# Triangular solves on VectorE alone, and 320 zero products left out, in a delta-rule attention and mixture-of-experts kernel

## The chip, the cores and the metric

One core of one Trainium2 chip. The metric is the device time in microseconds (us) of one execution, and the time of a kernel is the median of several. Engine names: PE is TensorE (PEld its weight loads), DVE is VectorE, ACT is ScalarE, POOL is GpSimd, SP is SyncE (SPq is its queue of DMA starts). L448 is line 448 of the kernel before; lines of the changed kernel are named as such.

## The reference

Three stages follow one another. First a delta-rule attention over 4 batches x 8 heads, 768 tokens, head size 48:

```
for t in range(S):
    y[:, :, t] = einsum('bhd,bhde->bhe', q[:, :, t], state)
    v_old = einsum('bhde,bhd->bhe', state, k_n[:, :, t])
    state = state + beta_t * einsum('bhd,bhe->bhde', k_n[:, :, t], v[:, :, t] - v_old)
```

`k_n` is `k` divided by its norm. Then its output (3072 tokens of 384) goes through a mixture of 8 experts with a greedy assignment (each expert takes 384 tokens; two products with a relu between), and last through a dense layer pair with `h * sigmoid(h)` between, 384 to 2048 to 384.

## The kernel before, in words

The attention is computed in 24 chunks of 32 tokens, all 32 heads together (4 blocks of 32 partitions x 8). Inside a chunk the recurrence over 32 tokens becomes a triangular system, whose inverse is computed for a group of 4 chunks at once. There are 6 groups (`GROUPS`), so 6 solves.

- `prep` (L371 loads, L373 on ACT, L374 on DVE, L379 DMAs within SBUF) and `gram` (L396 on PE, then L403 on ACT, L405 on DVE, L409 on ACT, and L410 on DVE or POOL) make a chunk's Gram matrices in high and low halves.
- `tgroup` makes a group's inverse: two transposes (L421), norms (L426 to L441, with two scalings by L439), the first values of X (L448), a mask and the diagonal (L451 and L454, always on POOL), and then 30 rounds of a multiplication (L462) and an addition (L465). Round j takes n columns of X by m = 31 - j elements, each instruction reads what the one before it wrote, and the columns are cut between DVE and POOL by the table `SPLIT`, so that each engine runs its own chain of 60 instructions (fewer on POOL). Two transposes (L468) end the solve, then L475 on ACT and L477 on DVE or POOL write the result for each of the 4 chunks. X and the temporary exist once, so solves follow one another.
- `stage(c)` loads chunk c's keys and values (L485), converts (L488 on ACT, L489 on DVE), scales the values (L492 on DVE or POOL), and moves all operands of the chunk within SBUF by four DMAs (L497) into one of two buffers `rsl`. It waits for the chunk's inverse.
- `step(c)` is the recurrence over chunks: PE products L519 (values), L527 (keys by state), L537 (queries by state), L548 (inverse), L563 (state), L574 (output), with L502 on ACT and L503 on DVE after the first, the inverse and the state product (5 L503 of a chunk), L507 to L510 for halves made by PE, and after every second chunk four DMAs L586 that write the output.
- `gate(c)` makes the gate's logits (L595, L599 or L600 and L602, L608, and L614 after chunk 19 and after chunk 23).

After the attention come the expert search (L924 to L1034) and the experts' products (`mm`, L1138).

The order of all instructions is set when the kernel is built, by a list scheduler (`Plan`): every operation has a cost and a priority, operations with two engines in their cost table (L410, L477, L492, L804 and others) are given to one of them, and each engine then runs its list strictly in that order. At the beginning `shapes` puts 320 products of zeros on PE in several shapes, and `warm` has 300 more products of zeros (L192) at the lowest priority, which the scheduler puts where it takes PE to be idle.

Of the kernel before, what the change touches and what calls it, by code (L numbers as in the profile page):

```python
# [20 lines left out]
C = 32  # L21
# [10 lines left out]
N6 = 3  # L32
FH = 0.0
KF = 2
SPLIT = (
    (("DVE", 0, 6), ("Pool", 6, C)),
    (("DVE", 0, 5), ("Pool", 5, C)),
    (("DVE", 0, 4), ("Pool", 4, C)),
    (("DVE", 0, 5), ("Pool", 5, C)),
    (("DVE", 0, 4), ("Pool", 4, C)),  # L40
    (("DVE", 0, 10), ("Pool", 10, C)),
)
GROUPS = tuple(tuple(range(c, c + 4)) for c in range(0, NCH, 4))
SX, SWG = 6, 10

# [143 lines left out]
def warm(P, nc, bank, z, n, r, w):  # L189

    for _ in range(n):
        P.op("PE", WC, lambda e: nc.tensor.matmul(bank[:, 0:256], z[:, 0:128], z[:, 128:], start=True, stop=True),  # L192
             r=r, w=w, prio=-1e6, look=(1.0, 0.0))


def shapes(P, nc, banks, z, r, w):

    T = nc.tensor
    forms = (
        (1, lambda i: (slice(0, 128), slice(0, 128), 0)),  # L200
        (2, lambda i: (slice(64 * i, 64 * i + 64), slice(64 * i, 64 * i + 64), 0)),
        (2, lambda i: (slice(64 * i, 64 * i + 64), slice(0, 128), i)),
        (4, lambda i: (slice(32 * i, 32 * i + 32), slice(32 * i, 32 * i + 32), 0)),
        (2, lambda i: (slice(0, 128), slice(64 * i, 64 * i + 64), 0)),
    )

    for n, (k, form) in enumerate(2 * forms):
        def go(e, n=n, k=k, form=form):
            for j in range(32):
                rows, cols, b = form(j % k)  # L210
                at = 48 * (j // k % 8)
                T.matmul(banks[b][cols, at:at + 48], z[rows, 0:cols.stop - cols.start], z[rows, 128:176], start=True, stop=True)
        P.op("PE", 1.0, go, r=r, w=w, prio=HOT)


class Arena:


# [43 lines left out]
def act(n, sb=True):  # L262
    return 0.055 + 0.00083 * n + (0.043 if sb else 0.0)
# [10 lines left out]
def attention(tc, P, ar, sh, kq, kv, bt, cst, idh, wg, xs):  # L274
    nc = tc.nc
    V, A, G, T = nc.vector, nc.scalar, nc.gpsimd, nc.tensor
    E = {"DVE": V, "Pool": G}
# [29 lines left out]
    wz = ar.new(["wz"], [384], F16)  # L307
# [14 lines left out]
    def sta(t, at, Q):  # L322
        return t[:, at, Q // 4].rearrange("p s (i q) -> p (s i) q", q=4)[:, :, Q % 4]
# [12 lines left out]

    P.op("DVE", 0.2, lambda e: V.memset(wz, 0.0), w=["wz"])
    P.op("Pool", 0.1, lambda e: G.memset(tiny, 1e-30), w=["tiny"])
    shapes(P, nc, ar.banks[4:6], wz, ["wz"], [("y", 0), ("y", 1)])
    warm(P, nc, ar.banks[5], wz, WARM, ["wz"], [("y", 1)])  # L340
    P.op("DVE", 4.3, fill(gsl, "p x c g s n -> p (x c g s n)"), w=["gsl"])
    for t, k in ((rsl[1][:, 0:8], 1), (rsl[1][:, 8:], 1), (rsl[0][:, 0:8], 0), (rsl[0][:, 8:], 0)):
# [40 lines left out]
    def gram(c):  # L383
# [8 lines left out]
        def mm(e, Q):  # L392
            n = 0
            for t in range(2):
                for a, b in P3:
                    T.matmul(gp_[:, Q], sta(gs[:, x], 2 * a + t, Q), cv[:, :, b, t, Q // 4, :, Q % 4], start=(n == 0), stop=(n == 5))  # L396
                    n += 1
# [15 lines left out]
    def tgroup(g):  # L413
# [24 lines left out]
        for k in range(2):  # L438
# [3 lines left out]
             r=["nb0"], w=["nb1"])  # L442
        parts = [(k, en, k0, k1) for k, (en, k0, k1) in enumerate(SPLIT[g])]
        xk = [("X", k) for k in range(2)]
# [61 lines left out]
    def split_pe(hi, lo, acc, ident, s, n, kp, kh, kl):  # L506
        P.op("ACT", act(n, False), lambda e: A.activation(hi, acc, AF.Copy, scale=s), r=[kp], w=[kh])  # L507
        P.op("PE", 0.01 + n / 2400, lambda e: T.matmul(acc, ident, hi, start=False, stop=True, skip_group_check=True),
             r=["idl", kh], w=[kp])
        P.op("ACT", act(n, False), lambda e: A.activation(lo, acc, AF.Copy, scale=s), r=[kp], w=[kl])  # L510

    def step(c):
        x = c % 2
        rs, y = rsl[x], yp[x]
        for g in range(2):
            w_, u_, n_, wu_, st_ = wt[g], ut[g], ns[g], wu[g], st[g]

            def vin(e, g=g, wu_=wu_):
                T.matmul(wu_[:, 0], ids, kr[x][:, 8 + 4 * g:12 + 4 * g, :], start=True, stop=(c == 0))  # L519

            P.op("PE", 0.38, vin, r=["ids", ("kv", x, 0)], w=[("wu", g)], prio=LEAD["vin"])
            if c:
                def kn(e, bs, last, g=g, wu_=wu_, n_=n_):
                    for a, b in bs:
                        for Q in range(4):
                            for t in range(2):
                                T.matmul(wu_[:, 0, Q], sta(rs, KR[x] + 2 * a + t, 4 * g + Q), n_[:, b, t, Q, :],  # L527
                                         start=False, stop=(last and (a, b) == P3[-1] and Q == 3 and t == 1))
# [178 lines left out]
HOT = 1000.0  # L707
# [511 lines left out]
def _program(ins):  # L1219
    import concourse.bacc as bacc  # L1220

    nc = bacc.Bacc("TRN2", target_bir_lowering=False, num_devices=1)
    d = {k: nc.dram_tensor(f"in_{k}", a.shape, mybir.dt.from_np(a.dtype), kind="ExternalInput").ap()
         for k, a in ins.items()}
    out = nc.dram_tensor("out_0", _OUT, F32, kind="ExternalOutput").ap()
    with tile.TileContext(nc) as tc, ExitStack() as ctx:
        dram = ctx.enter_context(tc.tile_pool(name="dram", bufs=1, space=DRAM))
        xs = dram.tile([NTOK, 2 * DM], F16, name="xs")
        plan = Plan()
        ar = Arena(ctx, tc, plan, 212832)  # L1230
        ar.at(210852)
        sh = shared_tiles(ar)
        ar.at(0)
        plan.base, plan.look = 9.0 * HOT, LOOK
        attention(tc, plan, ar, sh, d["kq"], d["kv"], d["bt"], d["cst"], d["idl"], d["wg"], xs)
        moe(tc, plan, ar, sh, xs, d["w1"], d["w2"], d["win"], d["wout"], d["mch"], out)
        with tc.manual_schedule():
            plan.emit()
    return nc
# [22 lines left out]
```

## Time and profile before

| what | us |
|---|---|
| median of 3 runs | 1064.65 (1058.99 to 1065.28) |
| profiled execution, its own time | 1064.36 |
| its span in the trace | 1062.7 |
| outside the span | 1.66 |
| DVE busy over the span | 719.7 (68%) |
| POOL busy over the span | 395.8 (37%) |
| PE busy over the span | 935.5 (88%) |

Busy time is of instructions that work; a share over the whole span mixes stages. The attention ends at about 376 us, and the search and the experts follow.

### The profile page before, as it was taken

How to read it: one execution, taken by the hardware profiler on the slowest of the kernel's cores; microseconds unless marked ns; L12 is line 12 of the kernel's file. 1: busy time of each engine (PE TensorE's matmuls, PEld its weight loads, DVE VectorE, ACT ScalarE, POOL GpSimd, SP SyncE). 2: the span in 40 equal slices, each digit the busy share in tenths (PEclk: the TensorE clock that was granted, in tenths of full speed). 3: DMA queues.
4: the chain of work that ended last, by engine and by line, in shares of the span. 5: the costliest groups of instructions: out<-in, count | busy, mean ns of one | idle time of the engine just before them, and what ended most of it. 6: DMA issues, size and time to landing. Idle time of an engine off the chain costs nothing.

```text
span 1062.7 us, 27011 instructions
## 1 busy us (share of the span) xinstructions
PE 935.5 (88%) x11073; PEld 676.6 (64%) x11073; DVE 719.7 (68%) x1852; ACT 491.1 (46%) x970; POOL 395.8 (37%) x515
## 2 busy tenths in 40 slices
PE   6987989988897831978998999998998999899997
PEld 6867889888887821544665565665665666566664
DVE  5898888888875587999558458558458457442250
ACT  4314446464555542656436337336336336742250
POOL 6578565747452253375204204203104103202011
PEclk9989899998988965898999999999999999999999
DMA  7428497877787736232203203103103104501000
GB/s 224 112 57 195 109 215 171 197 187 182 185 168 172 182 104 219 84 107 87 78 1 96 69 1 112 53 2 116 49 2 112 53 1 123 160 2 38 9 1 23
DMA packets 178796, 107.72 MB, mean 101 GB/s; under 512 B 141552, under 2 KB 162416, under 8 KB 178672
## 3 DMA queue, kind: packets, MB, share of 16 engines
q1 hardware_dynamic: 175600, 96.55, 35.3%
q0 software_dynamic: 3072, 9.44, 2.6%
q8 instruction: 87, 1.43, 0.5%
q14 instruction: 37, 0.30, 0.1%
HBM read 65.07 MB, written 9.44 MB: 70 GB/s over the span
## 4 chain that ended last, share of the span: by engine, by line
PE 56%; DVE 20%; DMA 9%; POOL 4%; issue 3%; SPq 3%; ACT 2%; POOLq 0%; DVEq 0%; ACTq 0%
PE bank L1138 44%; DMA sb<-sb 4%; PE bank L396 3%; SPq L497 2%; DVE sb L917 2%; DVE sb L465 2%; DVE sb L462 2%; PE bank L527 2%; DMA sb<-in_kv 2%; POOL sb L465 2%; POOL sb L462 1%; PE bank L537 1%; PE bank L563 1%; DMA sb<-in_kq 1%; DMA sb<-xs,sb 1%
## 5 line engine op out<-in xcount | busy, mean ns | idle before, releaser
L1138 PE MATMUL bank<-sb 128*128 128x384 f16 x3456 | 593.6, 330 | 0.0
L1138 PEld LDWEIGHTS <-sb 128*128 128x128 f16 x3456 | 328.4, 99 | 211.5 <-issue 11.8
L1178 POOL TENSOR_TENSOR sb<-sb 128x384 f16<-128x384 f32 x43 | 42.3, 984 | 301.3 <-ACT sb L1177 215.7
L1177 ACT ACTIVATE sb<-sb 128x384 f16<-128x384 f32 x128 | 66.3, 521 | 52.6 <-DVE sb L1175 51.5
L396 PE MATMUL bank<-sb 128*128 128x64 f16 x1152 | 75.4, 242 | 12.2 <-DVE sb L374 5.0
L396 PEld LDWEIGHTS <-sb 128*128 128x128 f16 x1152 | 72.4, 119 | 14.5 <-issue 14.2
L1175 DVE SCALAR_TENSOR_TENSOR sb<-bank,sb 128x384 f32<-128x384 f32 x128 | 69.7, 550 | 15.1 <-ACT sb L1174 14.7
L1174 ACT ACTIVATE sb<-bank 128x384 f32<-128x384 f32 x128 | 61.3, 480 | 33.0 <-PE bank L1138 32.2
L465 POOL TENSOR_TENSOR sb<-sb 128x126 f32<-128x126 f32 (+22 forms) x146 | 71.5, 489 | 11.0
L502 ACT ACTIVATE sb<-bank 128x192 f16<-128x192 f32 (+1 forms) x118 | 45.8, 391 | 59.0 <-PE bank L527 32.6
L503 DVE SCALAR_TENSOR_TENSOR sb<-bank,sb 128x192 f16<-128x192 f32 (+1 forms) x118 | 49.5, 428 | 32.2 <-ACT sb L502 31.9
L1178 DVE TENSOR_TENSOR sb<-sb 128x384 f16<-128x384 f32 x85 | 51.1, 605 | 26.5 <-ACT sb L1177 25.6
L462 POOL TENSOR_TENSOR sb<-sb 128x126 f32<-128x126 f32 (+22 forms) x146 | 64.9, 445 | 10.5
L527 PE MATMUL bank<-sb 128*128 128x48 f16 x1104 | 47.5, 198 | 23.5 <-DMA sb<-sb 22.6
L465 DVE TENSOR_TENSOR sb<-sb 128x30 f32<-128x30 f32 (+23 forms) x180 | 62.1, 345 | 3.3
L1187 POOL DMA_INDIRECT out<-sb x24 | 24.8, 1034 | 100.6 <-ACT sb L1185 81.9
L462 DVE TENSOR_TENSOR sb<-sb 128x30 f32<-128x30 f32 (+23 forms) x180 | 59.9, 333 | 3.0
L527 PEld LDWEIGHTS <-sb 128*128 128x128 f16 x1104 | 44.2, 118 | 27.6 <-issue 25.0
L1064 ACT ACTIVATE sb<-sb 128x768 f32<-128x768 f32 x56 | 46.6, 838 | 27.8 <-DMA sb<-in_w 25.7
L1149 DVE SCALAR_TENSOR_TENSOR sb<-bank,sb 128x384 f16<-128x384 f32 x64 | 35.5, 555 | 31.9 <-ACT sb L1148 31.6
L1148 ACT ACTIVATE sb<-bank 128x384 f16<-128x384 f32 x64 | 31.4, 490 | 51.7 <-PE bank L1138 44.7
L563 PE MATMUL bank<-sb 128*128 128x48 f16 x1104 | 47.4, 193 | 5.2 <-ACT sb L502 3.3
(158 smaller groups left out, 1498.4 us busy)
## 6 DMA issues: line engine op xcount, KB each, us to landing
sb<-sb SPq DMA_DIRECT2D x96, 256.0 KB, 5.5
sb<-in_w SPq DMA_DIRECT2D x64, 384.0 KB, 5.1
sb<-in_kq SPq DMA_DIRECT2D x40, 256.0 KB, 4.2
sb<-in_kv SPq DMA_DIRECT2D x24, 384.0 KB, 4.9
sb<-sb SPq DMA_DIRECT2D x48, 128.0 KB, 3.7
sb<-in_win SPq DMA_DIRECT2D x8, 768.0 KB, 5.6
sb<-in_wout SPq DMA_DIRECT2D x8, 768.0 KB, 5.8
xs<-sb SPq DMA_DIRECT2D x48, 96.0 KB, 3.5
```

Source lines behind the costliest of these rows:

```text
L396: T.matmul(gp_[:, Q], sta(gs[:, x], 2 * a + t, Q), cv[:, :, b, t, Q // 4, :, Q % 4], start=(n == 0), stop=(n == 5))
L462: P.op(en, cost[en](n * m), lambda e, x=x, t=t, j=j, n=n, m=m: E[e].tensor_tensor(t, L[:, j:j + 1, j + 1:].to_broadcast([128, n, m]), x[:, ...
L465: P.op(en, cost[en](n * m), lambda e, x=x, t=t, j=j: E[e].tensor_tensor(x[:, :, j + 1:], x[:, :, j + 1:], t, op=OP.add), r=[("tmp", en)], ...
L503: P.op("DVE", dve(n), lambda e: V.scalar_tensor_tensor(lo, src, s, hi, op0=OP.mult, op1=OP.subtract), r=[r, wh], w=[wl])
L527: T.matmul(wu_[:, 0, Q], sta(rs, KR[x] + 2 * a + t, 4 * g + Q), n_[:, b, t, Q, :], start=False, stop=(last and (a, b) == P3[-1] and Q == 3 ...
L563: T.matmul(st_[:, t, Q], sta(rs, nat(x, a, t), 4 * g + Q), u_[:, b, Q], start=(c == 0 and n == 0 and Q == 0 and t == 0), stop=False, skip_ ...
L1064: op("ACT", act(n), lambda e: A.activation(st3, st3, AF.Copy, scale=2.0 ** s), [], [("stg", i)])
L1138: T.matmul(bk[:, :N], lw(a), rw(b), start=(first and n == 0), stop=(last and n == 2))
L1174: op("ACT", act(N, False), lambda e, bk=bk, y=y: A.activation(sg[y], bk[:, :N], AF.Sigmoid, scale=s3), [kbk], [("sg", y)])
L1175: v(dve(N), lambda e, bk=bk, y=y: V.scalar_tensor_tensor(gf[y], bk[:, :N], s3 * 2.0 ** SG, sg[y], op0=OP.mult, op1=OP.mult), [kbk, ("sg", ...
L1177: op("ACT", act(N), lambda e, f=f, y=y: A.activation(gT[:, 0, f], gf[y], AF.Copy), [("gf", y)], [("gT", f, 0)])
L1178: op({"DVE": dve(N), "Pool": pool(N)}, 0, lambda e, f=f, y=y: EN[e].tensor_tensor(gT[:, 1, f], gf[y], gT[:, 0, f], op=OP.subtract), [("gf" ...
```

## The change

The table `SPLIT` gives all 32 columns of each solve to DVE. Each of the 6 solves is then one chain of 60 instructions on DVE; L448 becomes one instruction on DVE over 1024 elements, and L451 and L454 stay on POOL, one each per solve, over all columns. The call of `shapes` and the function are gone. Nothing else is edited.

```
-SPLIT = (
-    (("DVE", 0, 6), ("Pool", 6, C)),
-    (("DVE", 0, 5), ("Pool", 5, C)),
...
-)
+SPLIT = 6 * ((("DVE", 0, C),),)
...
-def shapes(P, nc, banks, z, r, w):
...
-    for n, (k, form) in enumerate(2 * forms):
-        def go(e, n=n, k=k, form=form):
-            for j in range(32):
-                rows, cols, b = form(j % k)
-                at = 48 * (j // k % 8)
-                T.matmul(banks[b][cols, at:at + 48], z[rows, 0:cols.stop - cols.start], z[rows, 128:176], start=True, stop=True)
-        P.op("PE", 1.0, go, r=r, w=w, prio=HOT)
...
-    shapes(P, nc, ar.banks[4:6], wz, ["wz"], [("y", 0), ("y", 1)])
     warm(P, nc, ar.banks[5], wz, WARM, ["wz"], [("y", 1)])
```

The scheduler works from these entries, so the rest of the attention's order moves too. By the two orders, POOL loses its 292 solve instructions and takes 27 operations from DVE: 10 of L410 (DVE had 14 and has 4), 11 of L477 (18, then 7) and 6 of L492 (7, then 1); three L804 go the other way. On PE all 300 products of `warm` now stand ahead of the first L548 of chunk 0; before, 76 of them stood behind it. From the end of the first expert's search on, DVE's lists in both kernels are the same. In the changed kernel every line from `attention` on is 28 lower: L497 is its L469, L503 its L475.

On SP, before the change, the operands of chunks 20 and 21 (the last two L497 here) stand ahead of the output of chunks 18 and 19 (the last L586):

```order
L485 DMA sb<-in_kv 128x768
L497 DMA sb<-sb 32x32x128 x4
L586 DMA xs<-sb 32x8x192 x4
L485 DMA sb<-in_kv 128x768
L497 DMA sb<-sb 32x32x128 x4
L801 DMA sb<-in_win 128x3x512
L485 DMA sb<-in_kv 128x768
L497 DMA sb<-sb 32x32x128 x4
L586 DMA xs<-sb 32x8x192 x4
```

With the change, at the same place (L469 are operands, those of chunks 20 and 21 are the eight in one row; L558 is output):

```order
L469 DMA sb<-sb 32x32x128 x4
L457 DMA sb<-in_kv 128x768
L469 DMA sb<-sb 32x32x128 x4
L558 DMA xs<-sb 32x8x192 x4
L457 DMA sb<-in_kv 128x768 x2
L558 DMA xs<-sb 32x8x192 x4
L469 DMA sb<-sb 32x32x128 x8
L773 DMA sb<-in_win 128x3x512
```

The output of chunks 18 and 19 has moved ahead of the operands of chunks 20 and 21.

On DVE, at the end of the last solve, before the change (L462 and L465 are the solve, L468 its closing transposes, L503 belongs to the steps; five of the L503 around here are chunk 19's):

```order
L503 SCALAR_TENSOR_TENSOR sb<-bank_65,sb 128x384
L465 TENSOR_TENSOR sb<-sb 128x10x3
L462 TENSOR_TENSOR sb<-sb 128x20
L465 TENSOR_TENSOR sb<-sb 128x10x2
L462 TENSOR_TENSOR sb<-sb 128x10
L465 TENSOR_TENSOR sb<-sb 128x10
L503 SCALAR_TENSOR_TENSOR sb<-bank_67,sb 128x192
L468 STREAM_TRANSPOSE sb<-sb 128x512 x2
L503 SCALAR_TENSOR_TENSOR sb<-bank_66,sb 128x384
L503 SCALAR_TENSOR_TENSOR sb<-bank_67,sb 128x192
L492 TENSOR_TENSOR sb<-sb 128x384
L489 SCALAR_TENSOR_TENSOR sb<-sb 128x4x96
```

With the change, at the same place (L434 and L437 are the solve, L440 the transposes, L475 the steps, L571 and L586 the gate):

```order
L461 SCALAR_TENSOR_TENSOR sb<-sb 128x4x96
L437 TENSOR_TENSOR sb<-sb 128x29x2
L434 TENSOR_TENSOR sb<-sb 128x30
L437 TENSOR_TENSOR sb<-sb 128x30
L475 SCALAR_TENSOR_TENSOR sb<-bank_65,sb 128x384
L440 STREAM_TRANSPOSE sb<-sb 128x512 x2
L475 SCALAR_TENSOR_TENSOR sb<-bank_66,sb 128x384
L571 COPY sb<-bank_72 96x4x4x32
L449 TENSOR_TENSOR sb<-sb 128x256
L464 TENSOR_TENSOR sb<-sb 128x384
L461 SCALAR_TENSOR_TENSOR sb<-sb 128x4x96
L571 COPY sb<-bank_72 96x4x4x32
```

Chunk 19's instructions have moved ahead: 99 of the steps' 118 stand before the last solve's transposes, where 95 stood, and the gate's copies for chunks 18 and 19 come before any instruction of chunk 20. At the transposes of the four solves before it the counts are 18 (before: 8), 37 (34), 58 (54) and 76 (73).

## Rows read from the trace of the kernel before

**Rows 1.** Busy time by engine in stretches of the span (instructions in brackets)

```profile
core 0: us, PE busy (x) PEld busy (x) DVE busy (x) ACT busy (x) POOL busy (x), PEclk, DMA share, GB/s
38.00:326.00 288.00, 252.81 (x5191) 239.25 (x5188) 244.68 (x650) 131.66 (x315) 180.95 (x346) 0.92 0.71 164
326.00:376.00 50.00, 41.75 (x1034) 39.91 (x1032) 26.66 (x51) 30.02 (x67) 16.49 (x13) 0.90 0.75 171
376.00:500.00 124.00, 72.29 (x574) 43.03 (x574) 114.09 (x237) 65.39 (x104) 64.18 (x36) 0.77 0.37 121
```

**Rows 2.** DVE by line from 38 to 326 us: busy, mean ns, idle before

```profile
L465 DVE TENSOR_TENSOR sb<-sb 128x30 f32<-128x30 f32 (+23 forms) x180 | 62.1, 345 | 3.3
L462 DVE TENSOR_TENSOR sb<-sb 128x30 f32<-128x30 f32 (+23 forms) x180 | 59.9, 333 | 3.0
L503 DVE SCALAR_TENSOR_TENSOR sb<-bank,sb 128x192 f16<-128x192 f32 (+1 forms) x96 | 40.2, 427 | 14.0 <-ACT sb L502 13.9
L374 DVE SCALAR_TENSOR_TENSOR sb<-sb 128x512 f16<-128x512 f32 x34 | 24.5, 722 | 11.4 <-ACT sb L373 9.9 <-DMA sb<-in_kq 1.4
...
L489 DVE SCALAR_TENSOR_TENSOR sb<-sb 128x384 f16<-128x384 f32 x19 | 12.2, 640 | 3.2 <-ACT sb L488 3.2
L477 DVE TENSOR_TENSOR sb<-sb 128x256 f16<-128x256 f32 x17 | 11.1, 669 | 0.0
L448 DVE TENSOR_TENSOR sb<-sb 128x160 f32<-128x160 f32 (+3 forms) x6 | 8.3, 1375 | 0.0
L439 DVE TENSOR_TENSOR sb<-sb 128x512 f32<-128x512 f32 x10 | 8.0, 806 | 0.0
L405 DVE TENSOR_TENSOR sb<-bank,sb 128x256 f32<-128x256 f32 x19 | 7.9, 418 | 2.6 <-PE bank L396 1.5 <-ACT sb L403 0.9
...
L410 DVE TENSOR_TENSOR sb<-sb 128x256 f16<-128x256 f32 x12 | 5.8, 484 | 0.3 <-ACT sb L409 0.3
L492 DVE TENSOR_TENSOR sb<-sb 128x384 f32<-128x384 f32 x6 | 3.4, 564 | 0.8 <-DMA sb<-in_kv 0.8
```

**Rows 3.** DVE in order of time, solve instructions with POOL idle

```profile
296.88 0.37 DVE L462 TENSOR_TENSOR sb<-sb 128x210 f32<-128x210 f32 x1
...
313.17 0.27 DVE L465 TENSOR_TENSOR sb<-sb 128x110 f32<-128x110 f32 x1
313.48 0.27 DVE L462 TENSOR_TENSOR sb<-sb 128x100 f32<-128x100 f32 x1
...
321.21 0.18 DVE L465 TENSOR_TENSOR sb<-sb 128x20 f32<-128x20 f32 x1
321.43 0.18 DVE L462 TENSOR_TENSOR sb<-sb 128x10 f32<-128x10 f32 x1
```

**Rows 4.** DVE in order of time, with POOL at work

```profile
80.00 0.68 DVE L465 TENSOR_TENSOR sb<-sb 128x58 f32<-128x58 f32 x1
...
100.08 0.48 DVE L465 TENSOR_TENSOR sb<-sb 128x85 f32<-128x85 f32 x1
...
316.47 0.82 DVE L465 TENSOR_TENSOR sb<-sb 128x70 f32<-128x70 f32 x1
```

**Rows 5.** POOL in order of time, beside rows 4

```profile
79.92 0.68 POOL L410 TENSOR_TENSOR sb<-sb 128x256 f16<-128x256 f32 x1 [0.30 <-ACT sb L409]
...
100.02 0.44 POOL L465 TENSOR_TENSOR sb<-sb 128x144 f32<-128x144 f32 x1
```

**Rows 6.** PE in order of time, at the beginning and between chunks 1 and 2

```profile
6.22 7.91 PE L212 MATMUL bank<-sb 128*128 128x48 f16 x320 [6.22 <-DVE sb L337]
23.26 6.13 PE L396 MATMUL bank<-sb 128*128 128x64 f16 x96 [2.74 <-DVE sb L405]
...
107.96 7.69 PE L192 MATMUL bank<-sb 128*128 128x256 f16 x57
```

**Rows 7.** SP's queue in order of time, from the last solve's end

```profile
327.18 4.38 SPq L497 DMA_DIRECT2D sb<-sb  x4
...
342.69 2.80 SPq L586 DMA_DIRECT2D xs<-sb  x4
```

More of the change, by code (lines that the diff above doesn't have):

```diff
@@ L34 @@
 KF = 2
-SPLIT = (
-    (("DVE", 0, 6), ("Pool", 6, C)),
-    (("DVE", 0, 5), ("Pool", 5, C)),
[L38 to L41, printed above, removed]
-)
+SPLIT = 6 * ((("DVE", 0, C),),)
 GROUPS = tuple(tuple(range(c, c + 4)) for c in range(0, NCH, 4))
@@ L193, in warm @@
              r=r, w=w, prio=-1e6, look=(1.0, 0.0))
-def shapes(P, nc, banks, z, r, w):
[L198 to L205, printed above, removed]
-    for n, (k, form) in enumerate(2 * forms):
-        def go(e, n=n, k=k, form=form):
-            for j in range(32):
-                rows, cols, b = form(j % k)
-                at = 48 * (j // k % 8)
-                T.matmul(banks[b][cols, at:at + 48], z[rows, 0:cols.stop - cols.start], z[rows, 128:176], start=True, stop=True)
-        P.op("PE", 1.0, go, r=r, w=w, prio=HOT)
 class Arena:
```

## The prediction

> **What bounds the kernel now.** I read the busy time by stretches first [rows 1]. The reader is to see that the change touches the first 376 us, and that in the long stretch of the solves (38 to 326 us, from the first L448 to the last L468) DVE works 244.7 of 288 us and POOL 181. PE is busy for 252.8 us there, but its products wait for one another through ACT and DVE, chunk by chunk, while the solves are one after the other on DVE's list. From 376 to 500 us DVE is busy for 114.1 of 124 us with the search, which the change leaves as it is; what the attention gains or loses should therefore arrive at the end nearly whole.
>
> The next view is DVE by line in the stretch [rows 2]. The 360 solve instructions are busy for 62.1 + 59.9 = 122.0 us, half of what DVE does, with 6.3 us of gaps in front of them. The whole gap time is 288 - 244.7 = 43.3 us; without those 6.3 us it is 37 us of waits, 13.9 us of them of L503 for ACT, which means for the steps, and 9.9 us of L374 for ACT's conversion of loaded keys and queries. So the stretch is DVE's work plus waits spread over it: 251 + 37.
>
> The third view puts DVE and POOL beside each other [rows 3 to 5]. A solve instruction of 110 elements takes 0.27 us while POOL is idle, one of 210 takes 0.37, one of 10 takes 0.18: about 0.16 us and 1 ns per element [rows 3]. With POOL's part of the solve running beside it, one of only 85 elements takes 0.48 us, as long as the POOL instruction (0.44 us) that started 0.06 us ahead of it [rows 4, 5]. The two engines take turns. The present split saves DVE elements, and it pays for them in turns.
>
> **The change part by part.** I count in the profiled execution, 1064.36 us with 1062.7 us in the span, 0.3 us below the median of the runs shown, so that a sum made against it can stand for the median.
>
> 1. The solves. Over 30 rounds j x (31 - j) sums to 4960 elements, twice 4960 for multiplication and addition, and there are 60 instructions as before. From start to start an instruction of 110 elements takes 0.31 us (313.17 to 313.48) and one of 20 takes 0.22 us (321.21 to 321.43) [rows 3], which is 0.20 us and 1 ns per element. A solve then takes 60 x 0.20 + 9.92 = 21.9 us, six take 131.5 us. Before it was 122.0 + 6.3 = 128.3 us [rows 2]. That is +3.2 us. Shapes up to 240 elements go a little beyond the 210 that rows 3 show. Bounds: the gap between one instruction's end and the next start is about 0.04 us, and where another instruction of the list fills it, up to 360 x 0.04 = 14.4 us come back (-11.2 us); above, +3.2 us, with POOL's remaining work counted below. I take +3.2 us, since the rows with no other instruction between are the nearest to a long chain.
>
> 2. Operations that go from DVE to POOL: 10 of L410 at 0.484, 11 of L477 at 0.669 and 6 of L492 at 0.564 us [rows 2] make 4.8 + 7.4 + 3.4 = -15.6 us.
>
> 3. What these cost as neighbours. An addition of 58 elements that started 0.08 us behind a POOL L410 of 0.68 us took 0.68 us; by the line of part 1 it would take 0.22, so 0.46 us are lost [rows 4, 5]; one of 70 elements took 0.82 us beside an L492, 0.6 us lost [rows 4]. These are the third and the last of 15 such meetings, among 24 POOL instructions of these three lines that ran inside the solves; the 15 lost 7.8 us, 0.52 each. For 27 more of them it makes 27 x 15/24 x 0.52 = +8.8 us. Bounds: 0, if they fall beside work that doesn't meet them, and 27 x 0.68 = 18.4 us, if each holds DVE up for the whole length of that L410 [rows 5].
>
> The rows show an instruction that waits to the end of the other engine's. [...]
>
> 4. Smaller pieces on DVE. L448 took 8.3 us for its six [rows 2] with at most 320 elements on DVE, beside POOL's own L448; alone, with 1024 elements, it is 0.16 + 1.02 = 1.2 us by rows 3, six make 7.1: -1.2 us. L439 (0.806 us on average) meets less of POOL: at 0.16 + 0.51 = 0.67 us ten of them make -1.4 us. Bounds for both together: 0 to -2.6 us. L451 and L454 on POOL stay in front of each solve as before, only in one piece.
>
> 5. Work that is moved ahead of the last L468: by the orders 4 more L503 (0.427), 4 more L374 (0.722), 2 more L489 (0.640), one more L405 (0.418): 1.7 + 2.9 + 1.3 + 0.4 = +6.3 us [rows 2], less two copies L599 of about 0.4 us: +5.5 us. Without it the same work would come later, so the lower bound is 0.
>
> Parts 1 to 5: 3.2 - 15.6 + 8.8 - 2.6 + 5.5 = -0.7 us. POOL gives up 136 us of work and DVE gains nothing from it, since DVE paid for the share in turns.
>
> 6. The 37 us of waits. I take them as unchanged. Half of them could go (-18 us), if longer solves leave the steps more time to be ready; a gain beyond that is excluded by the conversions' share, which hang on loads and not on the solves.
>
> 7. The end of the attention. The operands of chunk 20 started at 327.18 us, 1.2 us after the stretch of the solves, while the output of chunks 18 and 19 was started 15.5 us after that, at 342.69 [rows 7]. Now this output stands ahead on the same queue. Four DMA starts of it take 2.80 us [rows 7]; if chunk 19 is done in time, that is the whole price: +2.8 us. Bounds: 0, if the output is issued before the solve ends, and +15.5 us, if it becomes ready no earlier against the solve than now.
>
> 8. The 320 zero products cover PE from 6.22 to 14.13 us, and PE then stands idle for 2.74 us before 23.26, waiting for DVE [rows 6]. What hides their removal is the loading and converting of keys and queries, on which PE waits. The 52 warming products that now stand first take 52 x 7.69/57 = 7.0 us at the rate of the 57 in rows 6, less than the 7.9 us they replace. Value 0. [...]
>
> 9. The 57 warming products at 107.96 us stood for 7.69 us in front of chunk 1's L537 [rows 6], on which the state's conversion for chunk 2 waited. They go to the front. Chunk 2 can start up to 7.7 us sooner, but chunk 4 needs the second solve, which is on DVE's list and no shorter; I take 0, with -7.7 us as the other end.
>
> The sum is -0.7 + 2.8 = +2.1 us: 1066.5 us. The change moves work from an engine with time to spare to the one that sets the pace, and yet it comes out even.
>
> **The rivals.**
>
> *Faster.* DVE's waits shrink by half, since 76 warming products are no longer between the steps and each solve leaves steps time to be ready: 1066.5 - 18 = 1048 us. For it speaks that the largest wait is of L503 (13.9 us) [rows 2] and that steps in front of the second solve were late by the 7.69 us of rows 6; against it, that the 9.9 us of L374 hang on loads.
>
> *Slower by the order.* With the change, 99 and not 95 of the steps' conversions stand ahead of the last L468, the gate's copies for chunk 19 follow, and SP holds the operands of chunk 20 back behind the output of chunk 19. If the last solve is done and chunk 19 is not, everything waits for chunk 19: then the end of the attention is late by the 15.5 us between the two starts of rows 7, and not by 2.8, which gives 1066.5 + 12.7 = 1079 us. It decides from the point at which chunk 19's last conversion comes after the last solve addition. For it: before, chunk 19's conversions ran on behind the last solve. Against it: the steps begin with fewer warming products in their way.
>
> *Slower by POOL's neighbours.* Every one of the 27 operations holds DVE for its whole length: 18.4 in place of 8.8 us, 1076.1 us. Against it are the 9 of 24 without a meeting. [...]
>
> **How the numbers follow.** A measurement of this kernel can tell about 1% (10.6 us) from no change. Forecast 0.50, at 1066.5; faster 0.20; slower by the order 0.25; slower by neighbours 0.05. So faster by over 1% has 0.20, within 1% 0.50, and slower by over 1% 0.30. The range goes from 1047 (the faster case with a little of part 8) to 1090 (slower by the order, with the upper end of part 3 in addition: 1079 + 9.6 = 1088.6).
>
> **What would show it.** In the changed kernel, 360 solve instructions should be busy for about 118 us with 10 to 14 us of gaps, plus losses in some two thirds of the POOL operations beside them; DVE's busy time from the first solve to the last should stay within 10 us of 245 us; the last transposes (L440 there) should end between 318 and 336 us. The first L558 ahead of the operands of chunk 20 shows part 7: if the queue waits there for more than 3 us behind the last transposes, the rival of the order is at work. A DVE stretch under 275 us, or solve instructions that take 0.2 us for 80 elements, would prove me wrong on part 1 or 6.

## The result and the profile after

The changed kernel takes 1073.71 us (median of 4, 1072.11 to 1076.31), the kernel before 1063.36 us beside it (4, 1058.99 to 1065.28): a ratio of 1.0106 [1.0064, 1.0147]. The prediction said 1066.5 us, in a range of 1047 to 1090. The range holds; the forecast is 7 us short, and the outcome lies on the border between "within 1%" and "slower by over 1%".

By stretches of the span (the columns of [rows 1]) the changed kernel reads so; 345 us is the end of its last solve, which was 326 us before:

```profile
38.00:345.00 307.00, 253.10 (x5317) 240.64 (x5315) 236.81 (x626) 139.37 (x329) 54.84 (x62) 0.88 0.71 155
345.00:439.00 94.00, 45.95 (x998) 40.99 (x997) 65.37 (x154) 42.18 (x77) 30.61 (x21) 0.64 0.64 172
```

The solves' stretch is 19 us longer [rows 1], and yet DVE does less in it: 236.8 us for 244.7. What grew is idle time, 70.2 us for 43.3. The line groups of DVE in this stretch (as [rows 2]; L434 and L437 are the solve's multiplication and addition, L475 was L503, L346 was L374, L377 was L405) say where:

```profile
L434 DVE TENSOR_TENSOR sb<-sb 128x30 f32<-128x30 f32 (+9 forms) x180 | 66.7, 371 | 5.4 <-POOL sb L423 2.8
L437 DVE TENSOR_TENSOR sb<-sb 128x30 f32<-128x30 f32 (+9 forms) x180 | 63.5, 353 | 2.7
L475 DVE SCALAR_TENSOR_TENSOR sb<-bank,sb 128x192 f16<-128x192 f32 (+1 forms) x100 | 42.9, 431 | 25.5 <-ACT sb L474 25.1
L346 DVE SCALAR_TENSOR_TENSOR sb<-sb 128x512 f16<-128x512 f32 x35 | 26.5, 766 | 13.9 <-ACT sb L345 9.3 <-DMA sb<-in_kq 3.3 <-DMA xs<-sb 1.3
...
L377 DVE TENSOR_TENSOR sb<-bank,sb 128x256 f32<-128x256 f32 x19 | 8.0, 421 | 14.9 <-ACT sb L375 12.3 <-PE bank L368 2.5
L411 DVE TENSOR_TENSOR sb<-sb 128x512 f32<-128x512 f32 x10 | 6.8, 681 | 0.0
L420 DVE TENSOR_TENSOR sb<-sb 128x1024 f32<-128x1024 f32 x5 | 6.1, 1224 | 0.1
```

The 360 solve instructions take 130.2 us with 8.1 us of gaps, 138.3 in all, for 128.3 before. The waits of all the rest are 70.2 - 8.1 = 62.1 us, for 37 before. L475 waits 25.5 us (14.0 before), L377 14.9 (2.6), L346 13.9 (11.4) [rows 2].

One of these waits, in order of time. DVE (start, us, line, operation, count):

```profile
99.12 0.40 DVE L437 TENSOR_TENSOR sb<-sb 128x240 f32<-128x240 f32 x1
99.55 0.41 DVE L434 TENSOR_TENSOR sb<-sb 128x238 f32<-128x238 f32 x1
105.79 0.69 DVE L346 SCALAR_TENSOR_TENSOR sb<-sb 128x512 f16<-128x512 f32 x1 [5.83 <-ACT sb L345]
106.40 0.40 DVE L437 TENSOR_TENSOR sb<-sb 128x238 f32<-128x238 f32 x1
```

ACT, which DVE waits for, and SP's queue, which ACT waits for:

```profile
102.78 0.62 ACT L479 ACTIVATE sb<-bank 128x384 f16<-128x384 f32 x1 [4.39 <-PE bank L546]
105.12 1.28 ACT L345 ACTIVATE sb<-sb 128x512 f16<-128x512 f32 x2 [1.72 <-DMA sb<-in_kq]
```

```profile
96.23 4.76 SPq L351 DMA_DIRECT2D sb<-sb  x4
101.04 1.58 SPq L343 DMA_DIRECT2D sb<-in_kq  x3
```

The next solve instruction, L437 of 238 elements, needs nothing but the L434 that ended at 99.96. It stands on DVE's list behind an L346 whose load SP started only at 101.04, and so the solve stands still: DVE is idle for 5.83 us. The L437 doesn't overtake it: it starts after the L346, at 106.40.

Which marks moved: first and last start of the last transposes of a solve (L440), of the inverse's products (L520) and of the experts' products (L1110) in the changed kernel,

```profile
L440 DVE STREAM_TRANSPOSE sb<-sb x12: 997/1055/1140, 69.7 to 344.0; 128x512 f32<-128x512 f32 x12
L520 PE MATMUL bank<-sb x576: 183/191/244, 82.1 to 389.9; 128*128 128x48 f16 x192
L1110 PE MATMUL bank<-sb x3456: 322/326/528, 439.0 to 1063.4; 128*128 128x384 f16 x192
```

and in the kernel before (L468, L548, L1138):

```profile
L468 DVE STREAM_TRANSPOSE sb<-sb x12: 994/1112/1169, 71.4 to 324.8; 128x512 f32<-128x512 f32 x12
L548 PE MATMUL bank<-sb x576: 182/191/244, 84.8 to 373.5; 128*128 128x48 f16 x192
L1138 PE MATMUL bank<-sb x3456: 322/326/528, 426.1 to 1055.8; 128*128 128x384 f16 x192
```

The delay is 19.2 us at the last solve, 16.4 at the last chunk's inverse, 12.9 at the first product of the experts and 7.6 at their last.

### The profile page after: what moved, and what is told of

It is laid out like the page before. It is cut to its first block, busy times and chain, and to the rows that moved or that the text cites. A ratio compares the mean times of both kernels' runs of the same rounds, so it can differ in the third digit from the quotient of the medians.

```text
span 1070.4 us, 26061 instructions
## 1 busy us (share of the span) xinstructions
PE 925.3 (86%) x10753; PEld 669.8 (63%) x10753; DVE 707.3 (66%) x1828; ACT 491.7 (46%) x970; POOL 265.9 (25%) x229
## 4 chain that ended last, share of the span: by engine, by line
PE 55%; DVE 16%; DMA 14%; SPq 5%; issue 4%; ACT 3%; POOL 3%; POOLq 0%; DVEq 0%; ACTq 0%
PE bank L1110 40%; DMA sb<-sb 5%; SPq L469 3%; PE bank L368 3%; PE bank L499 2%; DMA sb<-in_kq 2%; DMA sb<-xs,sb 2%; DVE sb L889 2%; PE bank L509 2%; PE bank L185 2%; PE bank L535 2%; DMA out<-sb 1%; DMA sb<-in_w 1%; DVE sb L434 1%; DVE sb L437 1%
## 5 line engine op out<-in xcount | busy, mean ns | idle before, releaser
L1110 PE MATMUL bank<-sb 128*128 128x384 f16 x3456 | 587.3, 328 | 0.0
L1110 PEld LDWEIGHTS <-sb 128*128 128x128 f16 x3456 | 326.3, 98 | 207.5 <-issue 5.4
L368 PE MATMUL bank<-sb 128*128 128x64 f16 x1152 | 75.3, 242 | 16.9 <-DVE sb L346 10.6
L368 PEld LDWEIGHTS <-sb 128*128 128x128 f16 x1152 | 72.8, 120 | 19.0 <-issue 16.1
L499 PE MATMUL bank<-sb 128*128 128x48 f16 x1104 | 48.0, 200 | 32.5 <-DMA sb<-sb 28.9
L475 DVE SCALAR_TENSOR_TENSOR sb<-bank,sb 128x192 f16<-128x192 f32 (+1 forms) x118 | 50.5, 430 | 38.5 <-ACT sb L474 38.1
L434 DVE TENSOR_TENSOR sb<-sb 128x30 f32<-128x30 f32 (+9 forms) x180 | 66.7, 371 | 5.4 <-POOL sb L423 2.8
L499 PEld LDWEIGHTS <-sb 128*128 128x128 f16 x1104 | 44.7, 117 | 35.1 <-issue 29.3
L437 DVE TENSOR_TENSOR sb<-sb 128x30 f32<-128x30 f32 (+9 forms) x180 | 63.5, 353 | 2.7
L464 POOL TENSOR_TENSOR sb<-sb 128x384 f32<-128x384 f32 x23 | 20.4, 890 | 149.7 <-DMA sb<-in_kv 72.9
L345 ACT ACTIVATE sb<-sb 128x512 f16<-128x512 f32 x48 | 29.1, 626 | 56.8 <-DMA sb<-in_kq 35.4
L889 DVE TENSOR_TENSOR sb<-sb 128x192 f16<-128x192 f16 (+3 forms) x116 | 49.2, 458 | 1.1
L535 PEld LDWEIGHTS <-sb 128*128 128x128 f16 x1104 | 45.1, 118 | 7.2 <-issue 6.2
```

The costliest lines, as they stand in the source:

```text
L434: P.op(en, cost[en](n * m), lambda e, x=x, t=t, j=j, n=n, m=m: E[e].tensor_tensor(t, L[:, j:j + 1, j + 1:].to_broadcast([128, n, m]), x[:, ...
L437: P.op(en, cost[en](n * m), lambda e, x=x, t=t, j=j: E[e].tensor_tensor(x[:, :, j + 1:], x[:, :, j + 1:], t, op=OP.add), r=[("tmp", en)], ...
L475: P.op("DVE", dve(n), lambda e: V.scalar_tensor_tensor(lo, src, s, hi, op0=OP.mult, op1=OP.subtract), r=[r, wh], w=[wl])
L535: T.matmul(st_[:, t, Q], sta(rs, nat(x, a, t), 4 * g + Q), u_[:, b, Q], start=(c == 0 and n == 0 and Q == 0 and t == 0), stop=False, skip_ ...
L889: V.tensor_tensor(mv, a, iota2[:, None, 0:J].to_broadcast([128, h, J, 2]), op=o)
L1110: T.matmul(bk[:, :N], lw(a), rw(b), start=(first and n == 0), stop=(last and n == 2))
```

## The experiments

The change does three things at once: it moves the solves' work, it drops the products, and it makes the scheduler plan everything else anew. The first runs take these apart. Two theories stood against each other at the start: that the work costs (long solves on DVE, POOL operations beside them), or that the new order of the lists costs. All ratios are to the kernel before, run beside each.

**The work without the order, and the order without the work.** `e1_old_order`: the kernel before plans as it did, but when the instructions are written out, DVE's solve instructions take all columns and POOL's are left out.

```
-                P.op(en, cost[en](n * m), lambda e, x=x, t=t, j=j, n=n, m=m: E[e].tensor_tensor(
+                P.op(en, cost[en](n * m), lambda e, x=x, t=t, j=j, k=k, m=m: None if k else V.tensor_tensor(
```

> All solve columns on VectorE, but every engine's list in the order of the kernel before (the zero products included); GpSimd's solve instructions are gone. Three theories of the 10 us that the change cost. Order (the solves' last instructions are listed behind more of the steps, so that staging can't run beside a step): 1058 to 1068 us, the solve instructions of VectorE busy for about 120 us, waits of VectorE near 37 us as before. Work (the solves are longer on VectorE, and GpSimd's other operations hold it up): 1071 to 1077. Products (PE colder or the warming products in other places): 1058 to 1068, like order, since the products stand where they stood.

`e2_new_order_split`: the changed kernel plans as it does, but each solve instruction is written out as two, on DVE and POOL, by the table of before.

```
+WORK = (
+    (("DVE", 0, 6), ("Pool", 6, C)),
...
-                P.op(en, cost[en](n * m), lambda e, x=x, t=t, j=j: E[e].tensor_tensor(
+                P.op(en, cost[en](n * m), lambda e, pt=pt, j=j, m=m: [E[f].tensor_tensor(
...
+                    op=OP.mult) for f, x, t, q in pt], r=LL + [xk[k]], w=[("tmp", en)])
```

> The reverse: every engine's list in the changed kernel's order, but each solve instruction cut into a VectorE and a GpSimd part with the columns of the table before. Order: 1071 to 1082 us, with VectorE's waits as in the changed kernel (about 70 us). Work: 1060 to 1067. Products: 1071 to 1077.

e1 took 1060.49 us, 0.9967 [0.9946, 0.9988]: with before's lists the solves on DVE alone are 3.5 us faster. e2 took 1078.67 us, 1.0162 [1.0116, 1.0207]: the new lists are slow even when POOL does its old share of the solves. Both are what the order theory expected. The order costs, the work doesn't. (e2 doesn't bring back all of the earlier work: the 27 small operations stay on POOL and the 320 products stay out.) The groups of the solve in e1 (38 to 326 us):

```profile
L462 DVE TENSOR_TENSOR sb<-sb 128x30 f32<-128x30 f32 (+9 forms) x180 | 62.5, 347 | 3.0
L465 DVE TENSOR_TENSOR sb<-sb 128x30 f32<-128x30 f32 (+9 forms) x180 | 60.5, 336 | 3.3
```

They are as long as the split solve's [rows 2], with some 2.4 times the elements (9920 a solve, for 4070 where DVE had 5 columns).

**The products.** `e3_before_no_products` is the kernel before without the call of `shapes`, planned anew; `e4_after_with_products` is the changed kernel with it.

```
-    shapes(P, nc, ar.banks[4:6], wz, ["wz"], [("y", 0), ("y", 1)])
```

> The kernel before with the 320 zero products left out and nothing else edited (the scheduler moves some rows; at the ends of the solves 16, 36, 54, 73 and 95 of the steps' conversions come before, 8, 34, 54, 73 and 95 in the kernel before). Order: 1058 to 1070 us. Work: 1060 to 1066. Products: 1070 to 1077.

> The changed kernel with the 320 zero products put back (18, 38, 58, 76 and 99 conversions before the ends of the solves, as in the changed kernel but one). Order: 1070 to 1078 us. Work: 1070 to 1077. Products: 1060 to 1067.

e3 took 1052.52 us, 0.991 [0.9875, 0.9944]; e4 took 1083.35, 1.0189 [1.0152, 1.0226]. Both lie outside what any of the three theories expected, e3 below and e4 above: none of them had a gain from leaving the products out. Without the products either plan is 10 to 11 us better. Two more runs ask whether that is their execution. `e5_products_not_run` keeps before's lists and doesn't issue the 320 products:

```
-            for j in range(32):
+            for j in range(0):
```

> The kernel before with every list as it was, only that the 320 zero products are not issued (the scheduler still counts them). Place theory (the gain of leaving them out comes from where the scheduler then puts the 300 warming products, all ahead of the steps): 1060 to 1066 us, as before. Own-time theory (the products themselves delay something, or change PE's clock): 1050 to 1056 us.

`e6_57_fewer` keeps before's lists and doesn't issue the last 57 warming products, those of part 9:

```
+        if done[0] <= n - 57:
+            nc.tensor.matmul(bank[:, 0:256], z[:, 0:128], z[:, 128:], start=True, stop=True)
```

> The kernel before with every list as it was, only that the last 57 of the 300 warming products, those that stand ahead of chunk 1's L537, are not issued. Place theory: 1051 to 1058 us, with chunk 2 starting 6 to 12 us sooner than 121 us. Own-time theory: 1061 to 1066. If those products are needed to keep PE's clock up: over 1066.

e5: 1065.16 us, 1.0016 [0.9991, 1.0042]. e6: 1066.94 us, 1.0022 [1.0001, 1.0044]. Neither gains anything; for e5 the place theory had said so, for e6 it had expected 1051 to 1058. In e6 (lines 6 higher than before) PE comes early to chunk 1's L543, at 108.75 us where [rows 6] end at 115.65, and then waits for DVE:

```profile
108.75 1.05 PE L543 MATMUL bank<-sb 128*128 128x48 f16 x24
...
118.89 1.12 PE L533 MATMUL bank<-sb 128*128 128x48 f16 x24 [5.32 <-DVE sb L509]
```

```profile
117.36 1.03 DVE L474 STREAM_TRANSPOSE sb<-sb 128x512 f32<-128x512 f32 x1
118.32 0.52 DVE L509 SCALAR_TENSOR_TENSOR sb<-bank,sb 128x384 f16<-128x384 f32 x1
```

The conversion L509 of the state stands behind the last instructions of the second solve on DVE's list, and DVE works without a wait from 109.65 us up to it. A third expectation of e6, that these products keep PE's clock up, is borne out in part: from 116 to 126 us PE's granted clock is 0.50, after PE had waited from 113.57 to 118.89, and it is 0.92 there in the kernel before.

```profile
116.00:126.00 10.00, 5.96 (x111) 5.50 (x111) 9.46 (x18) 4.21 (x11) 5.75 (x10) 0.50 0.54 110
```

What the products' clock is worth against their time on PE wasn't measured apart; e6 shows that the two together come to nothing. In e3's own plan (lines 1 lower) the conversions of that chain stand among the instructions of the second solve, and chunk 2's keys (L526) and the first half of its inverse (L547) run without a wait (the second half waits 0.66 us):

```profile
104.62 1.77 PE L526 MATMUL bank<-sb 128*128 128x48 f16 x48
...
107.74 0.55 PE L547 MATMUL bank<-sb 128*128 128x48 f16 x12
```

The inverse started at 121.44 us before. So the products' worth is what the planner does without them. That leaving out the 57 products lets chunk 2 start sooner, which I held after e3, is refuted by e6: its inverse starts at 122.13 us.

**The place of the solve in the list.** The next form of the order theory was that the solve's end stands too late or too early among the steps. `e7_lead5` plans the changed kernel with a lead of 5 us for the solve in its priority:

```
-... "gram": 8.0, "tgroup": 0.0, "stage": -2.0, ...
+... "gram": 8.0, "tgroup": 5.0, "stage": -2.0, ...
```

> The changed kernel with the scheduler's lead of tgroup raised from 0 to 5, so that the ends of the solves stand behind 14, 34, 54, 70 and 94 of the steps' conversions in place of 18, 37, 58, 76 and 99. Order theory: 1048 to 1064 us, since staging runs beside the group's last step again, and the products are left out as well; chunk 4 to follow chunk 3 within 16 us (24 in the changed kernel). Work theory: 1071 to 1077, the work being the same.

1078.7 us, 1.0138 [1.0104, 1.0173]: no better, and the waits are still 61 us. This form falls.

**Both halves that pay.** `e8_both`: e3's plan, written out with all solve work on DVE as in e1.

> The kernel of e3 (products left out, table of columns as before in the scheduler) with all solve work on VectorE as in e1. If the two gains (11 us of e3, 3.5 us of e1) add: 1046 to 1051 us. If the solve's work matters only where the steps are late: 1051 to 1055.

1049.37 us, 0.9864 [0.9814, 0.9914]: the two gains add. It does the work that the changed kernel does (but POOL has 32 of the small operations, for 60 there), and is 24 us faster than it.

Two other causes for these 24 us can be looked up in the traces. PE's granted clock in the stretch of the solves is 0.88 in the changed kernel, 0.92 before and in e8. Without the warming products, a product takes 45.0 ns of busy PE there and 44.1 before (230.2 us for 5118, 216.8 for 4915), an estimate of about 4 us over the stretch. And the warming products all run ahead of the first inverse in the changed kernel; but e4 and, further on, e10, as slow as it or slower, have 25 and 43 of them behind it, and e8 has 10. What is left to explain is why the planner, told of the all-DVE solve, makes a worse list.

**The cost in the plan.** The scheduler counts a DVE instruction of n elements at 0.07 us + 1.04 ns n (`dve`). By this a solve takes 14.5 us of DVE in the changed kernel's plan (60 x 0.07 + 9920 x 0.00104), and 7.7 to 11.3 us in before's plan, where DVE's share is 4 to 10 columns and POOL's chain is planned beside it; on the chip it is 21.4 us before and 23.1 in the changed kernel, with the gaps. The plan further adds 0.127 us between two dependent instructions on DVE and 0.102 on POOL (`HOP`). With these, the whole chain of an all-DVE solve counts 22.1 us, about what it takes on the chip, and in before's plan POOL's chain beside 5 columns counts 20.6. So what the two plans count differently is DVE's time, much more than the length of the solve's chain. My theory now: the chains of the other operations are longer on the chip than in the plan, and in before's plan the solve's time on DVE is short by more than they are. Its instructions then lie thick between their links on DVE's list, and the links are ready when DVE comes to them. `e9_half_cost` plans the changed kernel with half the cost for the rounds:

```
-                P.op(en, cost[en](n * m), lambda e, x=x, t=t, j=j, n=n, m=m: E[e].tensor_tensor(
+                P.op(en, 0.5 * cost[en](n * m), lambda e, x=x, t=t, j=j, n=n, m=m: E[e].tensor_tensor(
```

> The changed kernel, with the cost at which the scheduler counts a round of the solve halved; work and engines are as in the changed kernel, only the order of the lists differs. Cost theory (the plan counts the all-DVE solve at nearly its real length and the short chains of the steps too short, so DVE's list is at their results too early): VectorE's idle time before the end of the last solve falls from about 70 us towards 40, and the time is 1048 to 1058 us. Rival (the plan's costs are not the cause, any order made for all-DVE solves waits as much): waits 60 to 75 us, time 1071 to 1077 us.

1042.39 us (1041.55 to 1042.77), 0.9817 [0.9784, 0.9849]: 31 us faster than the changed kernel by one number that no engine executes, and the best of all versions, beyond the 1048 to 1058 that the cost theory expected. Its solves' stretch ends at 305 us; the stretch, and the groups in it:

```profile
38.00:305.00 267.00, 238.38 (x5000) 227.85 (x4999) 234.72 (x624) 129.63 (x309) 50.45 (x57) 0.92 0.78 174
```

```profile
L434 DVE TENSOR_TENSOR sb<-sb 128x30 f32<-128x30 f32 (+9 forms) x180 | 62.9, 349 | 3.6 <-POOL sb L423 0.2
L437 DVE TENSOR_TENSOR sb<-sb 128x30 f32<-128x30 f32 (+9 forms) x180 | 61.5, 342 | 3.7
L475 DVE SCALAR_TENSOR_TENSOR sb<-bank,sb 128x192 f16<-128x192 f32 (+1 forms) x93 | 39.4, 428 | 6.7 <-ACT sb L474 6.1
L346 DVE SCALAR_TENSOR_TENSOR sb<-sb 128x512 f16<-128x512 f32 x34 | 25.8, 762 | 10.0 <-ACT sb L345 10.0
```

The work is that of the changed kernel, but for 7 conversions L475 that come after the solves and 7 small operations that the new plan gives to DVE (POOL has 53 of L382, L449 and L464, for 60). So those operations on POOL aren't what made the changed kernel slow. The waits are 267 - 234.7 - 7.3 = 25.0 us, for 62.1.

`e11_best_true_cost` goes the other way. It is e8 with DVE's solve instructions counted at what one takes from start to start in a chain, 22.3 us a solve. This is more than the measured length: the 0.20 us of [rows 3] hold the gap to the next dependent instruction, and the plan adds its 0.127 us per link again, which makes a chain of 29.9 us (22.1 in the changed kernel's plan, 14.9 in e9's):

```
-                P.op(en, cost[en](n * m), lambda e, ...
+                P.op(en, (0.2 + 0.00104 * j * m) if en == "DVE" else cost[en](n * m), lambda e, ...
```

> The version without the 320 products, with all solve work on VectorE and the lists planned as for the split solve (1049.37 us); here the solve's VectorE instructions are counted in the plan at their measured length, 0.2 us and 1.04 ns per element, about twice what the plan counted before. Work and engines are the same. Cost theory: VectorE's list again comes to the chains too early, waits of 60 us and more before the end of the last solve, time 1065 to 1080 us. Rival (the length at which the plan counts a solve doesn't matter): 1046 to 1053 us.

1134.3 us, 1.0686 [1.0611, 1.076], 85 us slower than e8, and beyond what I expected. (POOL has 43 of the small operations here, for 32 in e8.) DVE's waits up to the end of its last solve at 394 us (L502 was L503, L404 was L405; us in total, times, longest):

```profile
DVE sb L502 <- ACT sb L501: 53.6, 40, 4.5
DVE sb L404 <- ACT sb L402: 38.5, 11, 5.9
```

**One chain at its true length.** If the other chains are short in the plan, the cure could be to lengthen them. `e10_gram_cost` counts the changed kernel's gram products at their measured length (48 of L368 take 3.15 us, a piece of 12 so 0.79):

```
-            P.op("PE", 0.45, lambda e, Q0=Q0: (mm(e, Q0), mm(e, Q0 + 1)),
+            P.op("PE", 0.79, lambda e, Q0=Q0: (mm(e, Q0), mm(e, Q0 + 1)),
```

> The changed kernel, with the scheduler's cost of a chunk's gram products on TensorE raised from 0.45 to 0.79 us for each of its four pieces, which is their measured length. Cost theory: the waits of L377 (24 us idle in the changed kernel) fall below 8 us, and the time falls to 1060 to 1068 us. Rival: L377 stops waiting but the same time turns up in front of L475 and L346, and the time is 1071 to 1077 us.

1073.67 us, 1.0105 [1.007, 1.014], nothing gained. The expected wait is gone, and another stands in its place:

```profile
L346 DVE SCALAR_TENSOR_TENSOR sb<-sb 128x512 f16<-128x512 f32 x33 | 25.1, 765 | 26.1 <-ACT sb L345 26.1
...
L377 DVE TENSOR_TENSOR sb<-bank,sb 128x256 f32<-128x256 f32 x19 | 8.0, 421 | 3.6 <-ACT sb L375 2.7 <-PE bank L368 0.8
```

In the stretch of the solves L377 fell from 14.9 to 3.6 us (the 24 us of the expectation are of the whole span) and L346 rose from 13.9 to 26.1. Here the rival was right: mending this one chain alone gains nothing.

**How far it goes.** `e12_quarter_cost`: as e9, with 0.25 for 0.5.

> As the version with the halved cost of the solve's rounds (1042.39 us), with a quarter in place of the half: by the plan's formula (0.07 us and 1.04 ns per element) a solve then counts 3.6 us, where it counted 7.3 with the half, 14.5 in the changed kernel and 22.3 at its measured length. Cost theory: VectorE waits still less before the end of the last solve, 40 us or fewer, and the time stays on the good side, 1035 to 1050 us, since the chains of the steps, not the solve, are now what is put off. Rival (the half was a lucky order, and the time goes up and down with any change of the order): anything between 1040 and 1080, without relation to VectorE's waits.

1058.73 us, 0.9939 [0.9911, 0.9967]: outside the 1035 to 1050 us that the cost theory expected. DVE's waits up to the last solve's end (311 us) are 27.4 us, nearly as few as in e9, and the solves end early; but now the steps are what is late. From the last transposes to the first product of the experts it takes 112 us (310.1 to 422.5), for 101 in e9 (304.3 to 405.2). Of the three costs tried, the half is the best, between two losses; where the optimum lies wasn't tried, and how much of e9's gain over e8 is a lucky order isn't known.

All versions by the same views (waits: DVE's idle time from 38 us to the end of the last solve, less the gaps ahead of solve instructions):

| version | median us | waits, us | last transposes start | first product of the experts |
|---|---|---|---|---|
| e9, cost halved | 1042.4 | 25 | 304.3 | 405.2 |
| e8, no products, work on DVE | 1049.4 | 35 | 315.5 | 415.2 |
| e3, no products, split | 1052.5 | 35 | 316.9 | 415.0 |
| e12, cost quartered | 1058.7 | 27 | 310.1 | 422.5 |
| e1, old order, work on DVE | 1060.5 | 37 | 321.8 | 423.9 |
| before | 1063.4 | 37 | 324.8 | 426.1 |
| e5, products not run | 1065.2 | 38 | 326.8 | 429.0 |
| e6, 57 fewer | 1066.9 | 39 | 327.2 | 428.7 |
| e10, gram's cost | 1073.7 | 59 | 342.7 | 439.1 |
| after | 1073.7 | 62 | 344.0 | 439.0 |
| e2, new order, split | 1078.7 | 72 | 346.4 | 443.0 |
| e7, lead 5 | 1078.7 | 61 | 341.8 | 442.2 |
| e4, products kept | 1083.4 | 69 | 352.9 | 448.0 |
| e11, measured cost | 1134.3 | 116 | 393.2 | 494.0 |

But for e12, the time goes roughly with the waits; between neighbours in the table it doesn't (e7 waits as long as the changed kernel and takes 5 us more).

The plan itself had said most of this. The scheduler's own start of the last transposes, which each kernel works out when it is built, is 218.6 us for the kernel before, 211.5 for e3 and e8, 242.5 for the changed kernel, 206.7 for e9, 197.2 for e12 and 287.3 for e11. In all versions the chip is there 95 to 113 us later than the plan; the differences between the versions are those of the plan, within 12 us.

## Why the prediction was right and wrong, point by point

Parts 1 and 3, the solves and their neighbours: right. They promised 128.3 + 3.2 + 8.8 = 140.3 us for solve instructions and gaps, and it is 138.3. The turns of the two engines show as in [rows 4, 5]: a multiplication of 184 elements took 0.71 us beside a POOL L382 of 0.75, and the addition behind it 0.35 with POOL idle.

```profile
84.50 0.75 POOL L382 TENSOR_TENSOR sb<-sb 128x256 f16<-128x256 f32 x1 [4.80 <-ACT sb L381]
```

```profile
84.75 0.71 DVE L434 TENSOR_TENSOR sb<-sb 128x184 f32<-128x184 f32 x1
85.49 0.35 DVE L437 TENSOR_TENSOR sb<-sb 128x184 f32<-128x184 f32 x1
```

Part 3's upper bound of 18.4 us, in place of 8.8, would have made it 149.9 us; the trace lies below it, and in the kernel before 9 of the 24 POOL operations had met no solve instruction. e1 adds what the sum couldn't show: at before's order, which keeps the 27 operations on DVE, the work alone is worth -3.5 us, with 123.0 + 6.3 = 129.3 us of solves. And the neighbours' share hangs on the order: e9, with nearly as many operations on POOL, has 124.4 + 7.3 = 131.7 us.

Parts 2, 4 and 5: about right. L420 took 1.22 us (1.2 predicted), L411 0.681 (0.67), and 4 more L475 fell before the last solve's end, as the orders said (of 4 more L346 only 1 lies in the stretch). Parts 1 to 5 together promised -0.7 us of DVE's work in the stretch; it is 236.8 + 8.1 - 251.0 = -6.1, of which 1.2 us is the first L420, now before 38 us.

Part 6, the waits: this is the step that failed. "I take them as unchanged", with -18 us as the only other end. They went from 37 to 62.1 us, and +25.1 - 6.1 is the 19 us of the stretch. The last transposes ended at 345.0 us, outside the 318 to 336 that the prediction gave as its sign. I excluded a growth without a reason: I had read in the orders that 99 for 95 conversions stand ahead of the last solve's end, but took the lists for the same chain of events with other durations. DVE takes its list in order, as the 5.83 us ahead of that L346 show, and so the list itself is a cost. e2 shows that the list, with the solves split as before, costs 14.7 us (1078.67 against 1063.95). And the plan could have been asked: it moved the last transposes by 242.5 - 218.6 = 23.9 us, and the chip by 19.2.

Part 7, the output ahead of chunk 20's operands: right in kind. The last transposes ended at 345.0, the four output DMAs of chunks 18 and 19 started at 345.44 and the operands followed:

```profile
345.44 2.18 SPq L558 DMA_DIRECT2D xs<-sb  x4
347.72 10.06 SPq L469 DMA_DIRECT2D sb<-sb  x8
```

The operands start 2.7 us behind the transposes, where it was 1.2: +1.5 for the +2.8 predicted. The rival of the order, that all waits for chunk 19 here, didn't happen: the queue waited for 0.4 us. The side it forecast came true (1079 against 1073.7) by another mechanism, at six solves rather than at one place. So it is luck that the range, whose upper end came from this rival, reaches as far as the result.

Parts 8 and 9, the products: their execution is worth nothing, as both parts said (e5, e6). But leaving them out of the plan is worth 10 to 11 us (e3 against before, the changed kernel against e4), which neither part had. Part 9's lower end of -7.7 us comes near, but for PE's time on the 57 products, and e6 shows that this isn't the cause: DVE's list holds chunk 1's conversions behind the second solve. So the result is a sum of three, each shown by a pair of runs: -3.5 us for the work (e1), -11 us for the products' absence (e3), and +24 us for the plan of the all-DVE solve (the changed kernel against e8, the small operations on POOL included). They make +9.5 us, for the 10.3 measured; what this sum tests is that the first two add up in e8. That the forecast of +2.1 us came within 8 us of the result is luck too: the prediction had neither the -11 nor the +24, and they cancel in part. And of part 8's gain (7.0 us for 7.9), of which the range's lower end has a little, the traces show 0.2 us: the 52 warming products that now stand first took 7.75 us, at a granted clock of 1.00, for 7.91 of the zero products, also at 1.00.

"What the attention loses should arrive at the end nearly whole": wrong. Of 19.2 us, 7.6 arrived in the profiled run. 2.8 us came back in the steps behind the last solve, 3.5 in the search and 5.3 in the experts, of which below; between the medians 10.3 us are left.

What stays open: which links are short in the plan. That the cost at which the plan counts the solve's instructions on DVE decides is shown (e9, e11, with no other edit); whether by DVE's time or by the chain's length, which both hang on it, is not. That it does so because the other chains are counted short is argued from the waits and from one measured pair, gram's 0.45 for 0.79 us, and e10 shows that mending this one alone changes nothing.

## What to carry to other kernels

When a scheduler writes the lists, a change in who does the work is two changes: run the new work in the old order and the old work in the new order (e1, e2) before pricing either. Costs in a plan matter by their proportions: one entry raised to more than its length among others that are short (e11: 22.3 us of DVE a solve, for 7.7 to 11.3 in e8's plan) made the kernel 85 us slower, and the same entry halved (e9: 7.3, for 14.5 in the changed kernel's plan) gave the best version, 1042.39 us, faster than both kernels. Read the times that the scheduler itself gives to a mark on the way, here the last solve, before the kernel runs: their differences between versions came out on the chip within 12 us. A wait that is cured in front of one instruction should be looked for in front of the next (e10).

## What the runs showed of the hardware that was not expected

An instruction of another chain, between two that depend on each other, hid part of its cost. In the changed kernel, DVE in order of time:

```profile
120.28 0.32 DVE L434 TENSOR_TENSOR sb<-sb 128x168 f32<-128x168 f32 x1
120.53 0.34 DVE L403 RECIPROCAL sb<-sb 128x32 f32<-128x32 f32 x1
120.79 0.26 DVE L437 TENSOR_TENSOR sb<-sb 128x168 f32<-128x168 f32 x1
...
127.43 0.21 DVE L434 TENSOR_TENSOR sb<-sb 128x30 f32<-128x30 f32 x1
127.67 0.21 DVE L437 TENSOR_TENSOR sb<-sb 128x30 f32<-128x30 f32 x1
```

The reciprocal starts 0.07 us before the record of the multiplication ends, and the addition that depends on it 0.08 us before the reciprocal's; two dependent ones lie 0.03 us apart (127.43 + 0.21 to 127.67). The gaps in front of solve instructions came out at 8.1 us for the 10 to 14 predicted; how much of that this overlap gives wasn't worked out.

The 3456 products of the experts ran from 439.0 to 1063.4, in 624.4 us, in the changed kernel, and in 629.7 before, with the same list on DVE. Over these stretches PE was busy for 595.33 us after and 601.82 before, at a granted clock of 0.99 and 0.98:

```profile
439.00:1063.40 624.40, 595.33 (x4073) 360.13 (x4072) 381.02 (x1010) 292.79 (x532) 156.85 (x120) 0.99 0.19 59
```

```profile
426.00:1056.00 630.00, 601.82 (x4076) 362.62 (x4073) 385.03 (x1010) 292.90 (x532) 154.58 (x120) 0.98 0.18 57
```

That is 146.2 ns of busy PE per matmul after and 147.7 before. The 5.3 us thus lie in PE's own time and go with the granted clock; why the clock was a little higher in this execution isn't shown.
